# Threshold attention and two feed-forward layers: the first layer's activation as a maximum in its own step, with three h and five y banks, and weight blocks of the second layer decoded one stage later

## The chip, the cores and the metric

The kernel runs on one core of a Trainium2 chip. The metric is device time in microseconds (us) of one execution; lower is better. The kernel before was run three times: 1042.65, 1046.85 and 1047.65 us, so its median is 1046.85 us.

## The reference, cut to what matters

```python
# q, k, v: 4 x 8 heads x 576 x 64; tau = 0.02
scores = scale * q @ k.T
keep   = scores >= max(scores) - tau
x      = softmax(scores where kept) @ v              # 2304 tokens x 512

h = x @ w_in                                          # 512 -> 2048   (first layer)
g = where(h >= 1, h, where(h <= -1, 0, (h + 1)**2 / 4))
x = g @ w_out                                         # 2048 -> 512

h  = x @ w_in2                                        # 512 -> 1024   (second layer)
so = h * softmax(h)
x  = (layernorm(so) * g_ln) @ w_out2                  # 1024 -> 512
```

The four weight matrices arrive as 64-bit floats. The chip's engines work on 32 bits, so every block of 128 x 512 weights is first put together from its two 32-bit words ("decoded"). There are 48 such blocks: 16 of w_in and 16 of w_out of the first layer, 8 of w_in2 and 8 of w_out2.

## The kernel before, in words

Every product is made of two or three matmuls: a tensor is split into a high part (a copy in the matmul's own format) and a low part (the difference). So each activation costs a ScalarE copy for "hi" and a GpSimd subtraction for "lo" before TensorE may use it.

**Attention** (to about 414 us of the profile). The heads are worked in 16 pairs of 9 units each (`attention_unit`, L682); a string in `ORDER` (L68) fixes for each unit what is issued in which order: scores of a later pair ("S", L305) with their row maxima on VectorE (L318), the shifted scores again ("E", L378) with their exponential on ScalarE (L389), the mask on VectorE (L394), the split of the result (L402 ScalarE, L403 GpSimd), the product with v (L426). All loads and copies through DMA go through SyncE's one queue, in program order: `load_kq` (L219 to L229), `stack_k` (L285, L286, L289), `stack_q` (L293), `load_v` (L239, L245), `store_head` (L440, L441), and for batches that are done `load_recip` (L465) into one buffer, which waits for the `normalise` before it (L473). A pair's second head has its `stack_k` DMA in the pair's unit 0, its `stack_q` in unit 2 and its first scores in unit 4.

**Decoding jobs.** The letter "J" in a unit calls `jobs.step`. A job is a generator that does one piece of a block's work per step: load the raw words (L515, 512 KB, SyncE's queue), absolute value (L485, ScalarE), five VectorE instructions (L487, L490, L493, L497, L500), one GpSimd addition (L504). What follows depends on the kind. `to_sbuf` splits the block into hi and lo for TensorE (L531 ScalarE, L533 GpSimd). `to_dram` writes the decoded block to DRAM (L538), from where a later job reads it as plain 32-bit floats (L520, and L529 for w_out2). In the kernel before the attention runs 12 jobs, one begun every 9 units (`JOB_EVERY`) and at most two open at a time: the 8 blocks of the first layer's first quarter, and then rows 0 to 3 of w_out2 through `to_dram`.

**First layer** (about 414 to 832 us). The order is 4 groups of the hidden columns (g), 5 chunks of tokens (c; three of 512, two of 384), 4 steps each (jj): 80 steps n. In step n TensorE does the 12 matmuls of `moe1_in` into one h bank of PSUM, and the 12 of `moe1_out` of two steps before (`LAGO = 2`) into four y banks, one for each 128 output columns. Between them lies `moe1_act`, in two parts:

```python
nc.vector.tensor_scalar(cl, ps, 1.0, -1.0, op0=ALU.min, op1=ALU.max)                                  # L757
nc.scalar.activation(out=ps, in_=ps, func=ACTF.Relu, bias=mone[:, 0:1], scale=1.0)                    # L758
nc.scalar.activation(out=cl, in_=cl, func=ACTF.Square, bias=half[:, 0:1], scale=0.5)                  # L759
yield
nc.vector.tensor_tensor(cl, cl, ps, op=ALU.add)                                                       # L761
nc.scalar.copy(gh, cl)                                                                                # L762
nc.gpsimd.tensor_tensor(gl, cl, f32(gh), op=ALU.subtract)                                             # L763
```

The first part of step n is issued in step n; the second part is issued in step n + 1, behind the first part of that step (L1009). So gh and gl of step n - 2, which `moe1_out` (L779) reads in step n, are made in step n - 1, behind the clamp of step n - 1. In each step `jobs.step` is called up to twice, ahead of the clamp (L1006) and after `moe1_out` and the stores of y (L1028). The jobs of this stage are the next quarter's 8 blocks, then two further `to_dram` blocks (`plan`, L970): 10 in each of the first three groups, at most three open; the last group prepares the second layer's weights. `finish` empties the list at the end of each group.

**Second layer** (about 832 to 1037 us): `moe2_in` (L821) into two h banks, the norm (`moe2_ln`), a transposition through DRAM, and `moe2_out` (L932).

PSUM has eight banks: in the first layer four are a rotating set for h, four are y0 to y3.

Of the kernel before, what the change touches and what calls it, by code (L numbers as in the profile page):

```python
# [9 lines left out]
F32 = mybir.dt.float32  # L10
# [11 lines left out]
def kernel(  # L22
# [39 lines left out]
    T_A, T_B = -16, -10  # L62
    S_UNITS = (-10, -9, -7, -7, -6, -5, -4, -3, -3, -2)
    TURN_AT = 3
    JOB_EVERY = 9


    ORDER = (  # L68
# [51 lines left out]
    one = const.tile([P, 1], F32, name="one")  # L120
    half = const.tile([P, 1], F32, name="half")
    warm = const.tile([P, 1], F32, name="warm")
    mone = const.tile([P, 1], F32, name="mone")
    tau_sb = const.tile([P, 1], F32, name="tau_sb")
    tau_abs = const.tile([P, 1], F32, name="tau_abs")
    ntau = const.tile([P, 1], F32, name="ntau")
# [37 lines left out]

    def setup():
        nc.vector.memset(half, 0.5)
        nc.vector.memset(mone, -1.0)
        make_identity(nc, ident)
        nc.vector.memset(scale2[0:D], 1.0)
        nc.vector.tensor_scalar(  # L170
            scale2[D:P], tau_sb[D:P], 0.0, float(D) ** -0.5, op0=ALU.is_ge, op1=ALU.mult
        )
        nc.vector.tensor_scalar(ntau, tau_sb, -1.0, None, op0=ALU.mult)
        nc.vector.tensor_tensor(tau_abs, tau_sb, ntau, op=ALU.max)
        nc.vector.tensor_tensor(ntau, tau_sb, ntau, op=ALU.min)
# [364 lines left out]
    class Jobs:  # L540
# [2 lines left out]


        def __init__(self, todo, every, depth):
            self.todo, self.depth = [(t, every) for t in todo], depth
            self.live, self.now, self.next, self.begun = [], 0, 0, 0

        def add(self, todo, every):
            self.todo += [(t, every) for t in todo]  # L550

        def step(self, kinds="asb", many=1):
            for job in list(self.live):
                if job[1] > self.now or job[2] and (job[2] not in kinds or job[2] != "a" and many <= 0):
                    continue
                many -= job[2] in ("s", "b")
                n = next(job[0], None)
                if n is None:
                    self.live.remove(job)
                else:  # L560
                    job[1:3] = [self.now + n[0], n[1]]
            if self.todo and self.now >= self.next and len(self.live) < self.depth:
                make, every = self.todo.pop(0)
                g = make()
                n = next(g)
                self.live.append([g, self.now + n[0], n[1], self.begun])
                self.begun += 1
                self.next = self.now + every
            self.now += 1

        def finish(self):
            while self.todo or self.live:
                self.step()

    fine, WAIT, AFTER_ADD = [True], [4], [2]
# [59 lines left out]
    nc.scalar.activation(out=warm, in_=one, func=ACTF.Exp)  # L635
    load_kq(0)
    setup()
    jobs = Jobs(parts(("in1", 0), ("out1", 0)) + ahead_out2(0, 1, 2, 3), JOB_EVERY, 2)
    LAGV = 3
    first_, last_, pe_, act_, late_ = {}, {}, {}, {}, {}  # L640
    by_letter = {"F": first_, "L": last_, "P": pe_, "A": act_, "T": late_}
# [82 lines left out]
    def x_split(c, kk):  # L724
# [4 lines left out]
        nc.scalar.copy(hi, xv)  # L729
        (nc.gpsimd if c else nc.vector).tensor_tensor(lo, xv, f32(hi), op=ALU.subtract)  # L730

    h_ps = {}
    g_t = {}

    def moe1_in(c, j):
        hi, lo = wg_t["in1", j // JG]
        f = slice((j % JG) * P, (j % JG) * P + P)
        ps = ps_h.tile([P, T], F32, tag="h", name="h1")[:, 0 : size(c)]
        xh, xl = x_t[c]
        for kk in range(KD):  # L740
            for n, (a, m) in enumerate(((hi, xh), (lo, xh), (hi, xl))):
                nc.tensor.matmul(  # L742
                    ps,
                    lhsT=a[:, kk, f],
                    rhs=m[:, kk, :],
                    start=(n == 0 and kk == 0),
                    stop=(n == 2 and kk == KD - 1),
                )
        h_ps[c, j] = ps

    def moe1_act(c, j):
        n = size(c)
        ps = h_ps.pop((c, j))
        cl = g_p.tile([P, T], F32, tag="cl", name="cl", bufs=CL)[:, 0:n]
        gh = g_p.tile([P, T], F32R, tag="gh", name="gh", bufs=LAGO + 1)[:, 0:n]
        gl = g_p.tile([P, T], F32R, tag="gl", name="gl", bufs=LAGO + 1)[:, 0:n]
        nc.vector.tensor_scalar(cl, ps, 1.0, -1.0, op0=ALU.min, op1=ALU.max)  # L757
        nc.scalar.activation(out=ps, in_=ps, func=ACTF.Relu, bias=mone[:, 0:1], scale=1.0)  # L758
        nc.scalar.activation(out=cl, in_=cl, func=ACTF.Square, bias=half[:, 0:1], scale=0.5)  # L759
        yield  # L760
        nc.vector.tensor_tensor(cl, cl, ps, op=ALU.add)  # L761
        nc.scalar.copy(gh, cl)  # L762
        nc.gpsimd.tensor_tensor(gl, cl, f32(gh), op=ALU.subtract)  # L763
        g_t[c, j] = (gh, gl)
        yield
# [3 lines left out]
    def moe1_out(c, j):  # L769

        gh, gl = g_t.pop((c, j))
        hi, lo = wg_t["out1", j // JG]
        jj = j % JG
        if jj == 0:
            y_ps[c] = [ps_y.tile([P, T], F32, tag=f"y{d}", name="y1")[:, 0 : size(c)] for d in range(KD)]
        for d in range(KD):
            ds_ = slice(d * P, (d + 1) * P)
            for n, (a, m) in enumerate(((hi, gh), (lo, gh), (hi, gl))):
                nc.tensor.matmul(  # L779
                    y_ps[c][d],  # L780
                    lhsT=a[:, jj, ds_],
                    rhs=m,
                    start=(jj == 0 and n == 0),
                    stop=(jj == JG - 1 and n == 2),
                )
# [27 lines left out]
    def moe2_in(i):  # L813
        r = slice(i % YT * P, i % YT * P + P)
        yh, yl = (t[:, :, r] for t in x_t["y", i // YT])
        ps = [ps_h.tile([P, T], F32, tag="h", name="h") for g in range(2)]
        n = 0
        for kk in range(KD):
            for a, s in ((yh, 0), (yh, 1), (yl, 0)):
                for g in range(2):  # L820
                    nc.tensor.matmul(  # L821
                        ps[g], lhsT=a[:, kk, :], rhs=wg_t["in2", g][s][:, kk, :],
                        start=(n < 2), stop=(n >= 6 * KD - 2),
                    )
                    n += 1
        h2_ps[i] = ps
# [72 lines left out]
    def moe2_tr(i):  # L899
        _, so = ln_t.pop(i)  # L900
        t = wg_pool[1].tile([P, KD, 512], F32R, tag="wg", name="ln").rearrange("p k t -> p (k t)")
        hi, lo = t[:, 0:FF2], t[:, FF2 : 2 * FF2]
        for g in range(2):
            o = slice(T * g, T * g + T)
            ps = ps_y.tile([P, T], F32, tag=f"y{g}", name="lt")
            for f in range(KD):
                r = slice(f * P, f * P + P)
                nc.tensor.transpose(ps[:, r], so[:, T * g + f * P : T * g + f * P + P], ident)
            nc.scalar.copy(hi[:, o], ps)
            nc.vector.tensor_tensor(lo[:, o], ps, f32(hi[:, o]), op=ALU.subtract)  # L910
        lt_t[i] = [v.rearrange("p (f t) -> p f t", t=P) for v in (hi, lo)]
# [14 lines left out]

    def moe2_out(i):
        hi, lo = lt_t.pop(i)
        ps = ps_y.tile([P, DM], F32, tag=f"y{2 + i % 2}", name="o")
        terms = [(hi, f, m) for f in range(KF2) for m in range(2)] + [(lo, f, 0) for f in range(KF2)]  # L930
        for n, (a, f, m) in enumerate(terms):
            nc.tensor.matmul(  # L932
                ps, lhsT=a[:, f, :], rhs=wg_t["out2", f // 4][m][:, f % 4, :], start=(n == 0), stop=(n == len(terms) - 1)
            )
        o = g_p.tile([P, DM], F32, tag="cl", name="o", bufs=CL)
        nc.scalar.copy(o, ps)
        for r, rows in out_rows(i):
            nc.sync.dma_start(rows, o[r, :])
# [12 lines left out]
        if 0 <= u - NU + X_FIRST < KD:  # L951
            x_split(0, u - NU + X_FIRST)
    scores_ps.close()
    ps_h = ctx.enter_context(tc.tile_pool(name="ps_h", bufs=4, space=PSUM))
    for u in range(NU, NU + LAGV + 2):
        attention_unit(u)
        if u - NU in IN_EARLY:
# [6 lines left out]
    if RAW3:  # L964
# [3 lines left out]
    nc.sync.dma_start(g_sb, g_ln.rearrange("(f p) -> p f", p=P))  # L968
    order = [(g, c, jj) for g in range(NG) for c in range(NCH) for jj in range(JG)]
    plan = [  # L970
        parts(("in1", 1), ("out1", 1)) + ahead_out2(4, 5),
        parts(("in1", 2), ("out1", 2)) + ahead_out2(6, 7),
        parts(("in1", 3), ("out1", 3)) + ahead_in2(*IN2_AHEAD),
        parts(("in2", 0), ("in2", 1)),
        parts(("out2", 0)),
        parts(("out2", 1)),
    ]
    begin = {(0, 0, 2): 0, (1, 0, LAGO): 1, (2, 0, LAGO): 2, (3, 0, LAGO): 3, (3, 1, 0): 4, (3, 2, 0): 5}
    jobs = Jobs([], 0, 3)
    fine[0], WAIT[0], AFTER_ADD[0] = False, 2, 1  # L980
# [7 lines left out]
    for n in range(len(order) + LAGO):  # L988
# [3 lines left out]
        if n < len(order):  # L992
            g, c, jj = order[n]
            if order[n] in begin:
                if jj == LAGO:
                    jobs.finish()
                jobs.add(plan[begin[order[n]]], EVERY[begin[order[n]]])
            if (g, c, jj) == (0, 0, 2):
                recips(bl)
            if (g, c) == (0, 1):  # L1000
# [5 lines left out]
                jobs.step(many=9)  # L1006
            act.append(moe1_act(c, j))
            next(act[n])
        if 0 < n <= len(order):  # L1009
            next(act[n - 1])  # L1010
        go, co, jo = order[n - LAGO] if n >= LAGO else (0, 0, 0)
        if n >= LAGO:
            moe1_out(co, JG * go + jo)
# [12 lines left out]
            next(ln[i2])  # L1026
        if n < len(order):
            jobs.step(many=9)  # L1028
            if g == 0 and 4 < n <= 4 + NPAIR:
                normalise(bl, n - 5, nc.vector)  # L1030
            for m in range(x_done(n), x_done(n + 1)):
# [69 lines left out]
```

## Time and profile before

| | us |
|---|---|
| median of 3 runs (lowest, highest) | 1046.85 (1042.65, 1047.65) |
| the profiled execution, its own time | 1043.3 |
| its span, first to last instruction | 1041.5 |
| attention, 28.0 to 414.6: length, TensorE busy | 386.6, 347.84 |
| first layer, 420.2 to 832.0: length, TensorE busy | 411.8, 397.51 |
| second layer, 849.0 to 1037.0: length, TensorE busy | 188.0, 187.98 |

Length minus busy time is time in which TensorE had no matmul under way. In the attention that is 38.8 us, in the first layer 14.3 us, in the second layer 0.0. The profiled execution's own time is 1.8 us more than its span, and 3.55 us less than the median of the three runs.

### The profile page before, as it was taken

The page shows a single profiled execution, that of the slowest core. Times are in us where ns is not written, and L with a number is a line of the kernel's source. Part 1 is how long each engine was busy: PE and PEld are TensorE (multiplying, and loading weights), DVE is VectorE, ACT ScalarE, POOL GpSimd, SP SyncE. Part 2 cuts the span into 40 slices and gives each one's busy share as a digit, 9 for nine tenths or more (in the row PEclk, how much of TensorE's full clock was granted, in tenths as well). Part 3 has the DMA queues.
Part 4 walks back from the last instruction along what each step waited for, and adds up shares of the span by engine and source line. Part 5 has one row for each costly group of instructions (what it writes and reads, how often), then busy time and mean ns, then how long its engine had stood idle before and what let it go on. Part 6 is the DMA issues. An engine that isn't in the chain of part 4 may idle for free.

```text
span 1041.5 us, 15175 instructions
## 1 busy us (share of the span) xinstructions
PE 969.5 (93%) x5232; PEld 841.7 (81%) x5232; DVE 732.1 (70%) x1133; ACT 535.3 (51%) x1006; POOL 598.0 (57%) x569
## 2 busy tenths in 40 slices
PE   4899899889979998999999999999999999999998
PEld 3788888788878897767887888788888988888886
DVE  3788888868877775588747875787567556666662
ACT  2666666756756666645443443444344534344433
POOL 6577778967786776657524552555256823344332
PEclk9999999989999999999999999999999999999999
DMA  6555556555755520321121112111211104444443
GB/s 155 136 136 135 124 136 160 136 122 131 184 145 126 132 70 24 91 84 59 33 71 61 42 41 81 51 51 41 91 41 51 56 7 132 108 121 127 122 131 91
DMA packets 89885, 99.89 MB, mean 96 GB/s; under 512 B 50032, under 2 KB 62640, under 8 KB 89808
## 3 DMA queue, kind: packets, MB, share of 16 engines
q1 hardware_dynamic: 89424, 98.76, 36.5%
q8 instruction: 41, 0.67, 0.3%
q14 instruction: 36, 0.29, 0.1%
q10 hardware_dynamic: 384, 0.16, 0.1%
HBM read 55.13 MB, written 15.88 MB: 68 GB/s over the span
## 4 chain that ended last, share of the span: by engine, by line
PE 54%; issue 13%; DVE 12%; POOL 10%; ACT 6%; DMA 3%; SPq 2%; ACTq 0%; POOLq 0%; DVEq 0%
PE y L779 10%; PE h L742 10%; PE o L932 10%; PE h L821 9%; PE av L426 6%; PE zt L378 5%; PE sc L305 3%; DVE e L394 3%; POOL gl L763 3%; POOL dec_a L504 2%; POOL plo L403 2%; POOL wg L533 2%; ACT e L389 2%; DVE mcol L318 2%; DMA q_st<-lo 1%
## 5 line engine op out<-in xcount | busy, mean ns | idle before, releaser
L403 POOL TENSOR_TENSOR plo<-e,phi 128x576 fp32r<-128x576 f32 x144 | 206.2, 1438 | 80.7 <-ACT phi L402 79.5
L763 POOL TENSOR_TENSOR gl<-cl,gh 128x512 fp32r<-128x512 f32 (+1 forms) x80 | 96.9, 1211 | 189.4 <-ACT gh L762 156.0
L779 PE MATMUL y<-gh,wg 128*128 128x512 f32 (+1 forms) x640 | 187.6, 374 | 4.1 <-ACT gh L762 4.1
L742 PE MATMUL h<-xh,wg 128*128 128x512 f32 (+1 forms) x640 | 185.8, 371 | 2.0 <-DVE e L394 2.0
L394 DVE SCALAR_TENSOR_TENSOR e<-zt,ntau,e 128x576 f32<-128x576 f32 x144 | 116.6, 810 | 64.9 <-ACT e L389 64.7
L758 ACT ACTIVATE h<-h,mone 128x512 f32<-128x512 f32 (+1 forms) x80 | 49.5, 619 | 198.8 <-DVE cl L757 198.6
L389 ACT ACTIVATE e<-zt 128x576 f32<-128x576 f32 x144 | 93.7, 651 | 96.6 <-PE zt L378 81.1
L779 PEld LDWEIGHTS y<-gh,wg 128*128 128x128 f32 x640 | 117.9, 188 | 24.1 <-ACT gh L762 7.8
L742 PEld LDWEIGHTS h<-xh,wg 128*128 128x128 f32 x640 | 119.0, 189 | 19.2 <-DVE e L394 2.3
L779 PE MATMUL y<-gl,wg 128*128 128x512 f32 (+1 forms) x320 | 122.0, 381 | 10.2 <-POOL gl L763 10.2
L318 DVE TENSOR_REDUCE mcol<-sc 128x1 f32<-128x576 f32 x160 | 116.7, 747 | 10.4 <-PE sc L305 10.4
L757 DVE TENSOR_SCALAR cl<-h 128x512 f32<-128x512 f32 (+1 forms) x80 | 50.8, 635 | 102.0 <-PE h L742 69.0
L742 PE MATMUL h<-xl,wg 128*128 128x512 f32 (+1 forms) x320 | 118.8, 371 | 0.0
L932 PE MATMUL o<-wg,ln 128*128 128x512 f32 x432 | 103.2, 395 | 0.0
L821 PE MATMUL h<-wg,y 128*128 128x512 f32 x432 | 101.2, 390 | 0.0
L402 ACT CAST phi<-e 128x576 fp32r<-128x576 f32 x144 | 96.3, 669 | 2.1 <-DVE e L394 1.9
L932 PEld LDWEIGHTS o<-wg,ln 128*128 128x128 f32 x432 | 81.0, 188 | 19.2
L821 PEld LDWEIGHTS h<-wg,y 128*128 128x128 f32 x432 | 81.0, 188 | 17.0
L896 POOL TENSOR_TENSOR ln<-land,ln 128x1024 fp32r<-128x1024 f32 x16 | 38.5, 2408 | 92.2 <-ACT ln L895 86.4
L378 PE MATMUL zt<-q_st,k_both 128*128 128x288 f32 x320 | 76.9, 322 | 10.4 <-ACT mt L345 5.2
L305 PE MATMUL sc<-k_both,q_st 128*128 128x288 f32 x320 | 73.4, 312 | 13.1 <-DMA q_st<-lo 8.7
L779 PEld LDWEIGHTS y<-gl,wg 128*128 128x128 f32 x320 | 60.1, 188 | 27.3 <-POOL gl L763 19.1
(109 smaller groups left out, 1940.4 us busy)
## 6 DMA issues: line engine op xcount, KB each, us to landing
raw<-in_moe_w_in_dram SPq DMA_DIRECT2D x24, 512.0 KB
raw<-in_moe_w_out_dram SPq DMA_DIRECT2D x24, 512.0 KB
k_both<-q_st SPq DMA_DIRECT2D x30, 288.0 KB
sq<-so SPq DMA_DIRECT2D x64, 128.0 KB
land<-sq SPq DMA_DIRECT2D x16, 512.0 KB
k_both<-lo SPq DMA_DIRECT2D x32, 144.0 KB
q_st<-lo SPq DMA_DIRECT2D x32, 144.0 KB
x<-xs SPq DMA_DIRECT2D x32, 144.0 KB
```

Source lines behind the costliest of these rows:

```text
L305: nc.tensor.matmul(ps[:, c, 0:HS], lhsT=st[j][i][r, n * P : n * P + P], rhs=kk[j][i][r, o + c * HS : o + (c + 1) * HS], start=(st is q_st) ...
L318: nc.vector.tensor_reduce(mc[:, n : n + 1], sc_ps.pop((h, n))[:, :, 0:HS], axis=AXES.XY, op=ALU.max, negate=True)
L378: nc.tensor.matmul(ps[:, c, 0:HS], lhsT=st, rhs=mv[:, c * HS : (c + 1) * HS], start=(m == 0), stop=(m == len(todo) - 1),)
L389: nc.scalar.activation(out=e, in_=st_ps[u][:, :, 0:HS], func=ACTF.Exp)
L394: nc.vector.scalar_tensor_tensor(out=e, in0=st_ps.pop(u)[:, :, 0:HS], scalar=ntau[:, 0:1], in1=e, op0=ALU.is_ge, op1=ALU.mult)
L402: nc.scalar.copy(hi, e)
L403: (nc.vector if u - NU in LO_DVE or u < NU - UNITS and u % UNITS in LO_UNITS else nc.gpsimd).tensor_tensor(lo, e, f32(hi), op=ALU.subtract)
L742: nc.tensor.matmul(ps, lhsT=a[:, kk, f], rhs=m[:, kk, :], start=(n == 0 and kk == 0), stop=(n == 2 and kk == KD - 1),)
L763: nc.gpsimd.tensor_tensor(gl, cl, f32(gh), op=ALU.subtract)
L779: nc.tensor.matmul(y_ps[c][d], lhsT=a[:, jj, ds_], rhs=m, start=(jj == 0 and n == 0), stop=(jj == JG - 1 and n == 2),)
L821: nc.tensor.matmul(ps[g], lhsT=a[:, kk, :], rhs=wg_t["in2", g][s][:, kk, :], start=(n < 2), stop=(n >= 6 * KD - 2),)
L932: nc.tensor.matmul(ps, lhsT=a[:, f, :], rhs=wg_t["out2", f // 4][m][:, f % 4, :], start=(n == 0), stop=(n == len(terms) - 1))
```

## The change

In the first layer's activation the Relu and the addition become one maximum. The second part of the activation is issued at the end of its own step. The PSUM banks are split into three for h and five for y, and the y banks rotate: a chunk's four take the bank that was left free first. In the second layer an even tile takes one h and one y bank. The attention keeps only the 8 blocks of the first layer's first quarter, one begun every 14 units. The w_out2 blocks 0 to 3 are decoded in the first layer instead: its groups 0, 1 and 2 get lists of 3, 3 and 4 spare `to_dram` jobs behind the 8 that must be done, and `finish` no longer waits for spare jobs that are still open.

```diff
-    JOB_EVERY = 9
+    JOB_EVERY = 14
...
-            self.todo, self.depth = [(t, every) for t in todo], depth
+            self.todo, self.depth = [(t, every, True) for t in todo], depth
...
         def finish(self):
-            while self.todo or self.live:
+            while any(t[2] for t in self.todo) or any(job[3] for job in self.live):
                 self.step()
...
-    jobs = Jobs(parts(("in1", 0), ("out1", 0)) + ahead_out2(0, 1, 2, 3), JOB_EVERY, 2)
+    jobs = Jobs(parts(("in1", 0), ("out1", 0)), JOB_EVERY, 2)
...
+    NHB, NYB = 3, KD + 1
+    turns = [0, 0]
+
+    def bank(what, n, nm):
+        return (ps_h if what == "h" else ps_y).tile([P, T], F32, tag=f"{what}{n}", name=nm)
+
+    def y_bank(n, nm):
+        return bank("y", (turns[1] + n) % NYB, nm)
...
-        ps = ps_h.tile([P, T], F32, tag="h", name="h1")[:, 0 : size(c)]
+        ps = bank("h", turns[0] % NHB, "h1")[:, 0 : size(c)]
+        turns[0] += 1
...
         nc.vector.tensor_scalar(cl, ps, 1.0, -1.0, op0=ALU.min, op1=ALU.max)
-        nc.scalar.activation(out=ps, in_=ps, func=ACTF.Relu, bias=mone[:, 0:1], scale=1.0)
         nc.scalar.activation(out=cl, in_=cl, func=ACTF.Square, bias=half[:, 0:1], scale=0.5)
         yield
-        nc.vector.tensor_tensor(cl, cl, ps, op=ALU.add)
+        nc.vector.tensor_tensor(cl, cl, ps, op=ALU.max)
...
-            y_ps[c] = [ps_y.tile([P, T], F32, tag=f"y{d}", name="y1")[:, 0 : size(c)] for d in range(KD)]
+            y_ps[c] = [y_bank(d, "y1")[:, 0 : size(c)] for d in range(KD)]
+            turns[1] += KD
...
-        ps = [ps_h.tile([P, T], F32, tag="h", name="h") for g in range(2)]
+        ps = [bank("h", (turns[0] + n) % NHB, "h") for n in ((1, 2) if i % 2 else (0,))]
+        if i % 2 == 0:
+            ps.append(y_bank(0, "h"))
...
-        parts(("in1", 1), ("out1", 1)) + ahead_out2(4, 5),
-        parts(("in1", 2), ("out1", 2)) + ahead_out2(6, 7),
-        parts(("in1", 3), ("out1", 3)) + ahead_in2(*IN2_AHEAD),
+        parts(("in1", 1), ("out1", 1)),
+        parts(("in1", 2), ("out1", 2)),
+        parts(("in1", 3), ("out1", 3)),
...
+    spare = [ahead_out2(0, 1, 2), ahead_out2(3, 4, 5), ahead_in2(*IN2_AHEAD) + ahead_out2(6, 7), [], [], []]
...
+                jobs.add(spare[at_], EVERY[at_], False)
...
             act.append(moe1_act(c, j))
             next(act[n])
-        if 0 < n <= len(order):
-            next(act[n - 1])
...
         if n < len(order):
             jobs.step(many=9)
+            next(act[n])
```

## Rows read from the trace of the kernel before

**Rows 1.** The page: busy time, share of the span and instructions of each engine.

```profile
PE 969.5 (93%) x5232; PEld 841.7 (81%) x5232; DVE 732.1 (70%) x1133; ACT 535.3 (51%) x1006; POOL 598.0 (57%) x569
```

**Rows 2.** Windows: length, busy PE, PEld, DVE, ACT, POOL, granted clock, DMA share, GB/s.

```profile
28.00:414.60 386.60, 347.84 (x2383) 320.54 (x2384) 306.23 (x398) 253.13 (x480) 289.19 (x280) 0.98 0.53 127
420.20:832.00 411.80, 397.51 (x1861) 337.42 (x1861) 290.91 (x414) 185.55 (x338) 218.53 (x172) 1.00 0.19 59
849.00:1037.00 188.00, 187.98 (x826) 153.25 (x824) 113.82 (x276) 76.36 (x151) 63.84 (x49) 1.00 0.43 114
```

**Rows 3.** Waits of PE between 414 and 850 us: us, times, longest.

```profile
PE y L779 <- POOL gl L763: 10.2, 21, 0.9
PE y L779 <- ACT gh L762: 4.1, 9, 0.8
```

**Rows 4.** Timeline of one such wait: start, us, engine, line, [idle before].

```profile
498.39 0.55 DVE L487 TENSOR_SCALAR dec_a<-dec_a 128x512 f32<-128x512 f32 x1
...
503.27 0.69 DVE L500 SCALAR_TENSOR_TENSOR raw<-raw 128x512 f32<-128x512 uint32 x1
503.88 0.55 DVE L757 TENSOR_SCALAR cl<-h 128x384 f32<-128x384 f32 x1
...
504.47 0.56 ACT L758 ACTIVATE h<-h,mone 128x384 f32<-128x384 f32 x1 [3.71 <-DVE cl L757]
504.95 0.60 ACT L759 ACTIVATE cl<-cl,half 128x384 f32<-128x384 f32 x1
505.45 0.50 ACT L762 CAST gh<-cl 128x384 fp32r<-128x384 f32 x1
506.01 0.62 PE L779 MATMUL y<-gh,wg 128*128 128x384 f32 x2 [0.24 <-ACT gh L762]
...
507.09 0.44 PE L779 MATMUL y<-gl,wg 128*128 128x384 f32 x1 [0.47 <-POOL gl L763]
507.37 0.52 PE L779 MATMUL y<-gh,wg 128*128 128x384 f32 x2
507.72 0.34 PE L779 MATMUL y<-gl,wg 128*128 128x384 f32 x1
```

**Rows 5.** Windows of attention pairs, columns as in rows 2.

```profile
71.02:95.10 24.08, 21.89 (x154) 20.08 (x153) 20.86 (x27) 16.29 (x32) 18.59 (x18) 1.00 0.57 133
...
344.74:366.34 21.60, 20.37 (x149) 19.20 (x148) 15.78 (x22) 14.66 (x29) 15.22 (x16) 1.00 0.49 114
366.34:388.34 22.00, 20.67 (x149) 19.47 (x149) 16.72 (x23) 14.47 (x29) 15.76 (x16) 1.00 0.30 76
...
192.20:221.80 29.60, 24.37 (x155) 22.40 (x154) 19.18 (x28) 16.52 (x31) 21.40 (x22) 0.88 0.62 148
...
293.45:321.83 28.38, 23.28 (x155) 21.56 (x154) 19.23 (x27) 16.00 (x30) 20.17 (x21) 0.94 0.71 174
```

**Rows 6.** SyncE's queue, issues in order of time: start, us, line, transfer.

```profile
191.11 1.68 SPq L465 DMA_DIRECT2D rb<-rec  x2
...
199.21 0.53 SPq L515 DMA_DIRECT2D raw<-in_moe_w_out_dram  x1
199.83 0.65 SPq L285 DMA_DIRECT2D k_both<-q_st  x1
...
204.57 0.48 SPq L441 DMA_DIRECT2D x<-xs  x1
205.97 0.48 SPq L293 DMA_DIRECT2D q_st<-lo  x1
```

**Rows 7.** Windows at the two long waits and behind them, columns as in rows 2.

```profile
205.74:209.87 4.13, 0.00 (x2) 0.03 (x1) 1.41 (x2) 2.24 (x5) 3.46 (x3) 0.81 0.75 180
209.87:215.10 5.23, 5.23 (x22) 5.16 (x23) 1.51 (x2) 1.44 (x3) 1.38 (x5) 0.50 0.74 161
306.62:310.63 4.01, 0.00 (x0) 0.03 (x1) 1.60 (x2) 2.24 (x5) 3.38 (x4) 1.00 0.82 193
310.63:314.10 3.47, 3.47 (x15) 3.44 (x16) 0.76 (x1) 0.00 (x0) 1.62 (x4) 0.51 0.80 175
```

More of the change, by code (lines that the diff above doesn't have):

```diff
@@ L122 @@
     warm = const.tile([P, 1], F32, name="warm")
-    mone = const.tile([P, 1], F32, name="mone")
     tau_sb = const.tile([P, 1], F32, name="tau_sb")
@@ L166, in setup @@
         nc.vector.memset(half, 0.5)
-        nc.vector.memset(mone, -1.0)
         make_identity(nc, ident)
@@ L545, in __init__, with add @@
         def __init__(self, todo, every, depth):
-            self.todo, self.depth = [(t, every) for t in todo], depth
-            self.live, self.now, self.next, self.begun = [], 0, 0, 0
-        def add(self, todo, every):
-            self.todo += [(t, every) for t in todo]
+            self.todo, self.depth = [(t, every, True) for t in todo], depth
+            self.live, self.now, self.next = [], 0, 0
+        def add(self, todo, every, must=True):
+            self.todo += [(t, every, must) for t in todo]
         def step(self, kinds="asb", many=1):
@@ L562, in step @@
             if self.todo and self.now >= self.next and len(self.live) < self.depth:
-                make, every = self.todo.pop(0)
+                make, every, must = self.todo.pop(0)
                 g = make()
                 n = next(g)
-                self.live.append([g, self.now + n[0], n[1], self.begun])
-                self.begun += 1
+                self.live.append([g, self.now + n[0], n[1], must])
                 self.next = self.now + every
@@ L904, in moe2_tr @@
             o = slice(T * g, T * g + T)
-            ps = ps_y.tile([P, T], F32, tag=f"y{g}", name="lt")
+            ps = y_bank(1 + g, "lt")
             for f in range(KD):
@@ L928, in moe2_out @@
         hi, lo = lt_t.pop(i)
-        ps = ps_y.tile([P, DM], F32, tag=f"y{2 + i % 2}", name="o")
+        ps = y_bank(3 + i % 2, "o")
         terms = [(hi, f, m) for f in range(KF2) for m in range(2)] + [(lo, f, 0) for f in range(KF2)]
@@ L953 @@
     scores_ps.close()
-    ps_h = ctx.enter_context(tc.tile_pool(name="ps_h", bufs=4, space=PSUM))
+    ps_h = ctx.enter_context(tc.tile_pool(name="ps_h", bufs=1, space=PSUM))
     for u in range(NU, NU + LAGV + 2):
@@ L996 @@
                     jobs.finish()
-                jobs.add(plan[begin[order[n]]], EVERY[begin[order[n]]])
+                at_ = begin[order[n]]
+                jobs.add(plan[at_], EVERY[at_])
+                jobs.add(spare[at_], EVERY[at_], False)
             if (g, c, jj) == (0, 0, 2):
```

## The prediction

> **What bounds the kernel now.** I read the page first. TensorE (PE) is busy 93% of the span [rows 1], so the kernel can lose time only where PE waits, and the windows show where that is [rows 2]. The second layer has no gap: 187.98 us busy in 188.0. The change touches the order of its banks and nothing that PE waits for there, so I give it no part of the sum. The first layer has 411.80 - 397.51 = 14.3 us without a matmul, the attention 386.60 - 347.84 = 38.8 us.
>
> The waits say what ends the gaps of the first layer [rows 3]: 21 waits for gl (10.2 us) and 9 for gh (4.1 us), 14.3 us together, the whole gap. One of them in order of time shows why [rows 4]. Five VectorE (DVE) instructions of a decoded block run from 498.39 to 503.96. The clamp of step n stands behind them and starts at 503.88. The addition for step n - 1 stands behind that clamp, Relu and Square of step n stand ahead of the copy to gh on ScalarE (ACT), and so gh of step n - 1 comes at 505.45, when PE is done with all that it had. The value PE lacks is one whose inputs have been ready for a step; it waits in the queues behind work of the next step.
>
> For the attention I compared pairs of units [rows 5]. A pair with one block in decoding takes 24.08 us with DVE busy 20.86. The pairs at 344.74 and 366.34, after the last block, take 21.60 and 22.00 us with DVE busy 15.78 and 16.72. Two pairs are far longer, 29.60 and 28.38 us. In each of them PE stands still for about 4 us and then runs at a granted clock of 0.50 and 0.51 (1.2 GHz of 2.4) for 5.23 and 3.47 us [rows 7]. What comes late there is a stack DMA: SyncE's queue issues one DMA after the other from 191.11, when it came free of its wait for the normalised batch; a raw load (199.21) stands directly ahead of the stack of k (199.83), and the stack of q, which overwrites what that reads, goes out 6.14 us later at 205.97 [rows 6].
>
> **The change, part by part.**
>
> *Second part at the end of its own step, maximum, no Relu.* Issued in step n instead of n + 1, gh and gl have some 1.5 steps of PE's time until they are read, where they had one. In a chunk of 384 a step is about 4.2 us (24 matmuls, two of them in the 0.35 us between the starts of 507.37 and 507.72), so gh gains over 4 us against a lateness of 0.24 and 0.47 us in rows 4; the longest wait of the stage is 0.9 us [rows 3]. Relu (0.56 us in rows 4) leaves ACT's part of this chain; the maximum stands where the addition stood, and no row has one, so I bound it by the addition's cost (0 more) and one Relu (0.56 us more); either is inside the 4 us, and I take 0. The waits are 14.3 us. After each, the first matmuls are longer: 0.62 against 0.52 and 0.44 against 0.34 [rows 4], so 0.1 us for each of 30 waits, 3 us more. Upper bound 17.3 us. Lower bound 0, if DVE itself is what is late. I take three quarters, **-13 us**: the margin is several times the lateness, but DVE now holds a maximum that waits for Square, with the next step's decoding and clamp queued behind it, and PE waits for that clamp's result two steps on.
>
> *Banks.* The h bank of step n - 3 must be free in step n; its reader is now issued at the end of step n - 3, two steps ahead. The y banks' release appears in no wait of PE [rows 3], so the fifth brings 0. What hides a late release is the 2.1 us of `moe1_in` in front; if that cover goes, a store of y of about one Relu's length would be seen at 19 chunk changes, some 10 us, which the slower rival takes in.
>
> *Four blocks out of the attention.* For each: five instructions on DVE, one on ACT, one on GpSimd (POOL), a load and a store on SyncE's queue. Pairs with and without a block differ by 24.08 - 21.60 = 2.48 or 24.08 - 22.00 = 2.08 us [rows 5]. The later pairs also lack most of the loads of q and k, so 2.48 is the upper bound; the lower is 0, if those loads make all of it. DVE's difference of 4.1 to 5.1 us a pair speaks for decoding, so I take 1.9 a block: **-7.6 us** (0 to -9.9). The other 8 blocks stay, one every 14 units; I price them unchanged.
>
> *The two long pairs.* They exceed 24.08 by 5.5 and 4.3 us, 9.8 in all [rows 5], the bound. The jobs' new spacing puts loads at units 54 and 68 and none between, so the raw load of row 199.21 is gone, and in the second long pair, where a load begins in unit 96, the store of a decoded block and the load of unit 97 are gone. SyncE's queue is then about 0.6 us earlier in both, and 512 KB no longer stand ahead of the stack of k. I estimate the stack of q some 1.5 us earlier in each: its next limit is its place behind the rows of a finished head, which go out from 204.57 to 205.05 now [rows 6]. That is -3.1 us. The slow clock costs half of 5.23 and of 3.47 us, 4.3 in all [rows 7]. PE had stood still 2.5 us already when it fell in the first case (by its 0.81 in the window of the wait) and 4.0 in the second, so waits of 2.5 us lie between; I take a fifth, -0.9. Together **-4 us** (0 to -9.8).
>
> The Trainium skill says of this gate (TensorE: Matmul & The Clock Gate, What's actually happening) that "the default state is throttled, and activity releases the throttle", in words: the clock follows how busy PE has just been. By that a shorter wait could keep the full clock altogether, and the sum would be 3.4 us lower; no row here has a wait of that length.
>
> *Four blocks into the first layer.* DVE there is busy 290.91 of 411.80 us [rows 2]; by the pairs a block is at most 5.1 us, so 20 us more on 121 idle. What hides it is the new slack in the chain. They come behind each group's 8 needed blocks, and the needed ones begin when they began. 0 in the sum; up to +20 if the cover is gone.
>
> **The sum** is -13 - 7.6 - 4 = -24.6 us. The profiled execution took 1043.3, which gives 1018.7; it stands 3.55 below the median of 1046.85, from which the same gain gives 1022.2. I say 1020.
>
> **Rivals.**
>
> *One stage only.* The pairs' difference is the missing loads, or PE's earlier arrival turns into longer waits for the same DMAs: SyncE's chain from 191.11 hangs on POOL, not on PE [rows 6]. Then the attention gives about nothing and the first layer 13, or the other way round 11.6: about 1031. For it: two things changed between the pairs compared. Against it: DVE was fuller by just the block's work.
>
> *All of it.* -17.3 - 9.9 - 9.8 = -37: 1006. It needs both long waits short enough that the clock stays at 2.4 GHz. For it: PE never fell below it in the first layer, whose waits are at most 0.9 us. Against it: the queue's 5 us of lateness from 191.11 is not touched.
>
> *DVE becomes the bound of the first layer: slower.* Each of 80 steps now has one place where DVE stands still until Square is done, 0.60 us and two handings-over, say 0.8 us (an estimate from rows 4: 503.88 plus 0.55 to 504.47 and on): 64 us. With 20 us of decoding, 290.91 + 64 + 20 = 375 of the 397.5 us in which PE must work. It decides where decoding is dense enough for DVE to need more than PE in a stretch of several steps. If then the 20 us of the blocks come onto the path on top of the present waits, and the attention gives nothing, it is 1043 + 20 = 1063. Against it: most such halts are filled by the decoding issued between clamp and maximum.
>
> *Nothing gained.* The waits stay, with the maximum late in place of the addition, and the long pairs take what the four blocks leave: about 1043.
>
> **How the numbers follow.** Forecast 0.56, one stage only 0.22, all of it 0.12, nothing 0.06, slower 0.04. The range 1007 to 1035 takes in the forecast, one stage only, and part of the third. Half a per cent, about 5 us, is what a measurement of this kernel can tell from no change: faster by more 0.90, within it 0.06, slower 0.04.
>
> **What would show it.** Right: in the first layer the waits of PE for gh and gl under 5 us, and the stage from the first `moe1_out` to the second layer under 400 us; attention pairs of 22 to 23.5 us where none is long; the two waits near 2.5 us. Wrong: a wait of PE for gl that remains with DVE full, the pairs still 24 us, or the long waits unchanged with the slow clock behind them. The second layer should stay at 188 us.

## The result, and the profile after

The changed kernel takes 1006.96 us, median of four executions (1004.87 to 1010.71), against 1046.98 us for the kernel before in the same comparison: a ratio of 0.963 (95% interval 0.9588 to 0.9673), faster by 40 us. The forecast was 1020 with a range of 1007 to 1035, so the time lies at the low end of the range, 0.04 us outside it. The direction was right, and the size was 40 us where 24.6 were summed.

The page's line of busy time, after:

```profile
PE 962.0 (95%) x5232; PEld 850.7 (84%) x5232; DVE 711.2 (70%) x1132; ACT 499.3 (49%) x926; POOL 598.1 (59%) x569
```

PE's busy time fell by 7.5 us from [rows 1] for the same 5232 matmuls, the span by 32.6. Windows of the three stages after, columns as in rows 2:

```profile
28.00:405.30 377.30, 349.94 (x2392) 326.43 (x2393) 279.62 (x379) 250.14 (x476) 280.05 (x276) 0.99 0.53 122
410.90:800.50 389.60, 389.11 (x1862) 340.31 (x1861) 296.05 (x434) 154.02 (x264) 227.38 (x177) 1.00 0.23 70
817.50:1004.00 186.50, 186.50 (x825) 153.14 (x823) 113.58 (x276) 76.32 (x151) 63.79 (x49) 1.00 0.42 115
```

The first layer has 0.5 us left without a matmul; in [rows 2] it had 14.3. The wait of PE that is left and, below the dots, the wait of DVE that the change adds, between 410 and 800 us, after: us, times, longest:

```profile
PE y L788 <- POOL gl L771: 0.4, 1, 0.4
...
DVE cl L769 <- ACT cl L767: 23.4, 28, 1.2
```

Thirty waits have become one. The change also takes a wait of DVE away, one that the prediction did not count. There are two `cl` buffers, and with the second part issued a step late the clamp had to wait for the gl of an earlier step to be done with its buffer. DVE in the first layer before (420 to 832 us):

```profile
DVE cl L757 <- POOL gl L763: 24.2, 17, 2.2
```

After, there is no such wait in the stage: DVE stands still for Square 23.4 us, and no longer 24.2 us for gl. The timeline after shows a step in a chunk of 384 with a block in decoding, as in [rows 4] (start, us, engine, line, [idle before]):

```profile
480.16 0.54 DVE L766 TENSOR_SCALAR cl<-h 128x384 f32<-128x384 f32 x1
480.63 1.05 DVE L495 TENSOR_SCALAR raw<-dec_a 128x512 uint32<-128x512 uint32 x1
480.80 0.62 ACT L767 ACTIVATE cl<-cl,half 128x384 f32<-128x384 f32 x1 [2.77 <-DVE cl L766]
481.71 0.69 DVE L498 SCALAR_TENSOR_TENSOR raw<-raw 128x512 f32<-128x512 uint32 x1
482.32 0.55 DVE L769 TENSOR_TENSOR cl<-cl,h 128x384 f32<-128x384 f32 x1
482.96 0.52 ACT L770 CAST gh<-cl 128x384 fp32r<-128x384 f32 x1 [1.54 <-DVE cl L769]
483.55 1.02 POOL L771 TENSOR_TENSOR gl<-cl,gh 128x384 fp32r<-128x384 f32 x1 [2.16 <-ACT gh L770]
...
484.29 0.52 PE L788 MATMUL y<-gh,wg 128*128 128x384 f32 x2
...
484.64 0.43 PE L788 MATMUL y<-gl,wg 128*128 128x384 f32 x1
```

gl is complete at 484.57, and the first matmul that reads it begins at 484.64, 0.07 us later. In this step the margin of 4 us that the prediction counted on is used up: three instructions of the decoding had put the clamp off. Steps like this are few. When each of the 80 ends of gl is set against the first matmul that reads it, the median margin is 3.51 us, where it was 1.12 before; it is under 0.3 us in 3 steps (0.05, 0.06 and 0.07, all in the first group), where it was in 27. DVE does two instructions of the decoding between clamp and maximum, while Square runs, so here the maximum waits for nothing.

For the stages I set the first start of `moe1_out` and of `moe2_in` as borders. "After, again" is the same changed kernel in a later comparison (experiment 5). The profile of "after" is that of the slowest of its four executions (1010.71 us), the one of "after, again" that of the fastest of its four (1001.86).

| us | before | after | after, again | said |
|---|---|---|---|---|
| start to first `moe1_out` | 420.2 | 410.9 | 402.1 | -11.6 |
| to first `moe2_in` | 412.0 | 389.6 | 389.6 | -13 |
| to the end | 209.3 | 208.4 | 208.5 | 0 |
| span | 1041.5 | 1008.9 | 1000.1 | -24.6 |

The two profiles of the changed kernel differ in the attention alone, largely at its start: PE goes at about half its pace there in the one and not in the other (last section). Against the profile with a start like that of before, the stages gave -18.1, -22.4 and -0.9, together 41.4 us (the medians differ by 39 to 40).

The pairs of the attention, columns as in rows 5: an ordinary one and the two long ones, after:

```profile
80.43:102.91 22.48, 21.27 (x154) 20.01 (x153) 17.51 (x25) 15.19 (x29) 16.41 (x18) 1.00 0.60 140
...
171.25:197.86 26.61, 23.14 (x154) 21.52 (x153) 18.03 (x26) 16.34 (x31) 20.13 (x20) 0.94 0.60 136
...
288.22:314.48 26.26, 23.11 (x153) 21.44 (x152) 18.39 (x25) 16.39 (x31) 20.99 (x21) 0.94 0.61 143
```

Ordinary pairs went from about 24.08 [rows 5] to about 22.5 us. The long ones are shorter but there, and the first has come a pair earlier (it began at 192.20, now at 171.25). What holds it is again the stack of q, after, SyncE's queue in order of time:

```profile
175.38 1.10 SPq L463 DMA_DIRECT2D rb<-rec  x2
176.54 0.58 SPq L513 DMA_DIRECT2D raw<-in_moe_w_out_dram  x1
177.21 0.25 SPq L438 DMA_DIRECT2D sums<-xs  x1
177.50 0.48 SPq L439 DMA_DIRECT2D x<-xs  x1
178.03 0.59 SPq L291 DMA_DIRECT2D q_st<-lo  x1
```

and the windows of the two waits and of what follows each, after, columns as in rows 7:

```profile
181.13:183.50 2.37, 0.00 (x1) 0.03 (x1) 1.60 (x3) 2.24 (x5) 1.74 (x3) 1.00 1.11 218
184.60:188.02 3.42, 3.42 (x17) 3.39 (x16) 1.28 (x2) 1.62 (x3) 2.54 (x6) 0.50 0.46 110
298.01:300.08 2.07, 0.01 (x2) 0.04 (x1) 0.82 (x1) 1.94 (x4) 2.07 (x3) 1.00 0.83 227
300.65:304.06 3.41, 3.41 (x17) 3.36 (x15) 0.76 (x1) 0.66 (x2) 2.38 (x5) 0.50 0.82 181
```

The waits are 2.37 and 2.07 us long (4.13 and 4.01 in [rows 7]), and a stretch at 0.50 of the clock still follows each.

### The profile page after: what moved, and what is told of

It reads as the page before. It is cut to its first block, busy times and chain, and to the rows that moved or that the text cites. A ratio compares the mean times of both kernels' runs of the same rounds, so it can differ in the third digit from the quotient of the medians.

```text
span 1008.9 us, 15104 instructions
## 1 busy us (share of the span) xinstructions
PE 962.0 (95%) x5232; PEld 850.7 (84%) x5232; DVE 711.2 (70%) x1132; ACT 499.3 (49%) x926; POOL 598.1 (59%) x569
## 4 chain that ended last, share of the span: by engine, by line
PE 81%; ACT 5%; DVE 4%; issue 3%; POOL 3%; SPq 2%; DMA 1%; ACTq 1%; POOLq 0%; DVEq 0%
PE y L788 19%; PE h L750 19%; PE o L943 10%; PE h L832 10%; PE av L424 8%; PE zt L376 7%; PE sc L303 5%; DVE e L392 3%; ACT e L387 2%; PE tr L260 2%; POOL plo L401 1%; ACT phi L400 1%; ACTq L344 1%; DMA q_st<-lo 1%; ACT mt L343 1%
## 5 line engine op out<-in xcount | busy, mean ns | idle before, releaser
L771 POOL TENSOR_TENSOR gl<-cl,gh 128x512 fp32r<-128x512 f32 (+1 forms) x80 | 100.1, 1251 | 168.8 <-ACT gh L770 89.8
L767 ACT ACTIVATE cl<-cl,half 128x512 f32<-128x512 f32 (+1 forms) x80 | 54.4, 680 | 98.0 <-DVE cl L766 97.6
L770 ACT CAST gh<-cl 128x512 fp32r<-128x512 f32 (+1 forms) x80 | 46.3, 579 | 112.4 <-DVE cl L769 102.0
```

## The experiments

Runs 1 to 4 share one series of the kernel before (median 1044.64), 5 to 8 another (1044.96), 9 and 10 a third (1045.0), 11 and 12 a fourth (1045.45). Ratios are to these.

**1. The order alone**, in the kernel before.

```diff
-        if 0 < n <= len(order):
-            next(act[n - 1])
...
             jobs.step(many=9)
+            next(act[n])
```

> The kernel before with one edit: the second part of the activation is issued at the end of its own step (Relu and addition stay, banks and jobs stay). Theory: the place of issue alone takes TensorE's waits for gh and gl away: under 2 us of them left, 17 to 22 us less than the kernel before, all in the first layer. Rival (the Relu on ScalarE is the late link): waits stay above 8 us, at most 7 us less. Rival (banks): nothing gained, within 3 us of before.

Measured: 1025.3 us, 0.9817 (0.9792 to 0.9842). The first layer takes 392.4 us, 19.6 less. PE's waits there:

```profile
PE y L779 <- ACT x L794: 2.3, 2, 1.4
PE y L779 <- POOL gl L763: 0.3, 1, 0.3
```

The waits for gh and gl are gone but for 0.3 us. What is left hangs on ScalarE, which still does the Relu: it is late with the copy that empties a y bank.

**2. The maximum alone**, still one step late, in the kernel before.

```diff
-        nc.scalar.activation(out=ps, in_=ps, func=ACTF.Relu, bias=mone[:, 0:1], scale=1.0)
...
-        nc.vector.tensor_tensor(cl, cl, ps, op=ALU.add)
+        nc.vector.tensor_tensor(cl, cl, ps, op=ALU.max)
```

> The kernel before with one edit: no Relu, a maximum in place of the addition, still issued one step later. Theory (place of issue): gh still waits behind the next step's clamp and Square but comes some 0.6 us earlier, and most waits are 0.2 to 0.9 us, so a part goes: waits of 14.3 us fall to 4 to 9 us, 6 to 13 us less. Rival (Relu is the late link): all waits go, 17 to 22 us less. Rival (maximum slower than the addition): within 3 us of before or slower.

Measured: 1033.36 us, 0.9891 (0.9865 to 0.9917). The first layer takes 400.2 us, 11.8 less, with these waits:

```profile
PE y L778 <- POOL gl L762: 5.7, 14, 0.8
PE y L778 <- ACT gh L761: 0.2, 1, 0.2
```

Each edit alone takes over half the gain, and the two overlap: 19.6 + 11.8 = 31.4 against 22.4 in the whole change (which has new banks and four more blocks in this stage besides).

**3. The jobs alone**: blocks moved and spaced as in the change, with the old activation and banks.

```diff
-    JOB_EVERY = 9
+    JOB_EVERY = 14
...
-    jobs = Jobs(parts(("in1", 0), ("out1", 0)) + ahead_out2(0, 1, 2, 3), JOB_EVERY, 2)
+    jobs = Jobs(parts(("in1", 0), ("out1", 0)), JOB_EVERY, 2)
...
+    spare = [ahead_out2(0, 1, 2), ahead_out2(3, 4, 5), ahead_in2(*IN2_AHEAD) + ahead_out2(6, 7), [], [], []]
```

> The kernel before with the jobs of the change alone: 8 blocks in the attention, one every 14 units, the other four as spare jobs in the first layer; activation and banks as before. Theory: attention pairs 22.5 us instead of 24.1, the two long pairs some 3 us shorter each, 10 to 15 us less in the attention; the first layer's chain has no slack there, so its waits grow by 1 to 4 us with four more blocks; 8 to 13 us less in all. Rival (the pairs differ by the missing loads of q and k, not by decoding): pairs stay near 24, at most 4 us less.

Measured: 1038.12 us, 0.9942 (0.9917 to 0.9967), 6.5 us less. The first layer takes 421.5 us, 9.5 more than before. The waits there, and then a window with one of the longer ones (1.64 us for gh, ending at 817.17) and what follows it:

```profile
PE y L778 <- POOL gl L762: 12.6, 26, 0.9
PE y L778 <- ACT gh L761: 6.8, 12, 1.6
```

```profile
815.00:822.00 7.00, 4.89 (x20) 4.25 (x19) 4.01 (x9) 4.31 (x9) 3.58 (x4) 0.76 0.15 37
```

Four blocks in the first layer cost 9.5 us under the old order, in longer waits and one stretch below full clock. This misses the expectation, and it is the price of the cover that the prediction named.

**4. The whole change without the new banks** (four h banks, y0 to y3 fixed).

```diff
-        ps = bank("h", turns[0] % NHB, "h1")[:, 0 : size(c)]
+        ps = ps_h.tile([P, T], F32, tag="h", name="h1")[:, 0 : size(c)]
...
-            y_ps[c] = [y_bank(d, "y1")[:, 0 : size(c)] for d in range(KD)]
+            y_ps[c] = [ps_y.tile([P, T], F32, tag=f"y{d}", name="y1")[:, 0 : size(c)] for d in range(KD)]
```

> The whole change but for the banks: four h banks that rotate and y0 to y3, as before. Theory: banks give nothing, so 37 to 41 us less than the kernel before, as the changed kernel. Rival (rotating y banks free TensorE at chunk changes): 3 us or more short of the changed kernel, with waits of TensorE for the stores of y.

Measured: 1009.52 us, 0.9679 (0.9646 to 0.9711), 35 us less than before, a little short of what was expected. The first layer takes 390.1 us, 0.5 more than with the banks, and the second 209.3. Here too PE has one wait for gl, 0.4 us, in the first layer.

**5 to 8.** The changed kernel again, as the base of the next three (its diff is empty); a block every 9 units; the loads of the reciprocals later; two more blocks in the first layer.

> The changed kernel itself, on the chip of the three runs beside it, as their measure: 36 to 41 us less than the kernel before.

Measured: 1005.76 us, 0.9621 (0.9585 to 0.9656). Its first long wait is of interest: 2.10 us for the same stack of q, but the clock stayed full. The second is 2.11 us long and the clock fell. Windows of this run, the first wait with what follows, then the second, columns as in rows 7:

```profile
175.20:177.30 2.10, 0.01 (x1) 0.03 (x1) 1.61 (x3) 1.96 (x5) 1.47 (x2) 1.00 1.11 220
177.30:185.00 7.70, 7.20 (x51) 6.79 (x52) 4.38 (x6) 3.70 (x8) 7.55 (x9) 1.00 0.32 72
290.92:293.03 2.11, 0.00 (x0) 0.03 (x1) 0.82 (x1) 1.98 (x5) 2.11 (x3) 0.94 0.83 210
293.03:296.45 3.42, 3.42 (x15) 3.39 (x16) 0.76 (x1) 0.26 (x1) 2.89 (x5) 0.54 0.83 181
```

**6. A block every 9 units** in the changed kernel: eight blocks, as dense as before.

```diff
-    JOB_EVERY = 14
+    JOB_EVERY = 9
```

> The changed kernel with one block begun every 9 units again in the attention (8 blocks, so the last load is in unit 61 and not 96). Theory as predicted (every block costs its pair about 1.9 us, whatever the spacing): the pairs with a block go back to 24.1, those behind them to 22, the sum stays: within 3 us of the changed kernel. Rival (a pair has slack, and at one block in 14 units decoding fits into it, at one in 9 it does not): 7 pairs at 24.1 against 22.5, the rest 22.4 at the best: 7 to 12 us more than the changed kernel.

Measured: 1015.57 us, 0.9713 (0.9683 to 0.9742), 9.8 more than the change. Windows of a pair with a block, and of one behind the last block that still has its loads of q and k:

```profile
78.81:102.89 24.08, 21.91 (x153) 20.09 (x153) 20.86 (x27) 16.29 (x31) 18.58 (x19) 1.00 0.56 134
...
274.77:297.16 22.39, 21.17 (x154) 19.99 (x153) 15.55 (x22) 15.20 (x29) 18.06 (x18) 1.00 0.53 127
```

The pair is back at 24.08 us. Without decoding and with the loads it is 22.39: a block at that density costs 1.7 us, and the rest of the 2.48 and 2.08 us in the prediction was the loads missing from the two later pairs of [rows 5]. An ordinary pair of the changed kernel takes 22.48, 0.1 more. A few take longer (23.6 at the most), so the price is better taken from the sum: from the third pair to the fourteenth, without the two long ones, run 5 has 4.2 us more than 22.39 a pair, some 0.5 for each of the eight blocks if they make all of it.

**7. The loads of the reciprocals later**, so that SyncE's queue does not wait for them ahead of the next heads' stacks.

```diff
-    NORM = (13, 5)
+    NORM = ((15, 9), (15, 9), (16, 5))
...
-            o = (b + 1) * NPAIR * UNITS + NORM[0] + NORM[1] * p
+            o = (b + 1) * NPAIR * UNITS + NORM[b][0] + NORM[b][1] * p
...
-            at(late_, o + NORM[1], normalise, b, p, nc.vector if b == 2 else nc.gpsimd)
+            at(late_, o + NORM[b][1], normalise, b, p, nc.vector if b == 2 else nc.gpsimd)
```

> The changed kernel with the loads of the reciprocal sums moved: for the first two batches one every 9 units, in the unit of the load of q and k and behind it in SyncE's queue, for the third one every 5 units from 3 units later. Theory (the long pairs come from SyncE's queue standing at the reciprocal load ahead of the loads of q, k and the stacks): both long pairs fall from 26.5 to about 22.8 us, the waits for q_st and the half clock behind them go, 6 to 9 us less than the changed kernel. Rival (bandwidth of the DMAs, or GpSimd's normalising, is what is late): the long pairs only move or stay, within 2 us of the changed kernel.

Measured: 995.56 us, 0.953 (0.95 to 0.9559), 10.2 less than the change in the same comparison; the profiled executions differ by 6.2. It is the fastest version of this study. SyncE's queue and the window of the pair in which the first long wait was:

```profile
160.51 1.24 SPq L463 DMA_DIRECT2D rb<-rec  x2
...
164.29 0.64 SPq L283 DMA_DIRECT2D k_both<-q_st  x1
...
167.17 0.58 SPq L513 DMA_DIRECT2D raw<-in_moe_w_out_dram  x1
...
171.19 0.54 SPq L291 DMA_DIRECT2D q_st<-lo  x1
```

```profile
161.90:184.40 22.50, 21.23 (x153) 19.84 (x152) 17.86 (x24) 15.97 (x31) 17.70 (x18) 1.00 0.64 157
```

What SyncE's queue waited for at the load of the reciprocals, between 28 and 405 us, in the changed kernel and, in a second fence, in this run:

```profile
SPq L463 <- POOL x L471: 13.9, 5, 4.7
```

```profile
SPq L463 <- POOL x L471: 3.3, 3, 1.8
```

No pair is long any more. The raw load is still there, 4 us ahead of the stack of q, and every block's load with it; what this run changes is the hold of the queue at the reciprocals, which falls from 13.9 to 3.3 us on GpSimd, and that is the cause. The edit does two things at once, though: the loads stand elsewhere in the queue, and the normalising that they wait for comes every 9 units and not every 5 (for the first two batches). Which of the two shortens the hold was not tried apart, and neither was what a raw load close ahead of the stack of q adds to it.

**8. Two more blocks in the first layer** (rows 0 and 3 of w_out2 are decoded twice).

```diff
-    spare = [ahead_out2(0, 1, 2), ahead_out2(3, 4, 5), ahead_in2(*IN2_AHEAD) + ahead_out2(6, 7), [], [], []]
+    spare = [ahead_out2(0, 1, 2, 0), ahead_out2(3, 4, 5, 3), ahead_in2(*IN2_AHEAD) + ahead_out2(6, 7), [], [], []]
```

> The changed kernel with two blocks more in the first layer: rows 0 and 3 of w_out2 are decoded and stored twice, as spare jobs of the first two groups. Theory (the new slack hides decoding there): TensorE's waits in the stage stay under 1 us, at most 2 us more than the changed kernel. Rival (a block costs the first layer what it cost with the old order, 9.7 us for four when the jobs alone were moved): 4 to 6 us more.

Measured: 1009.65 us, 0.9668 (0.9636 to 0.97), 3.9 more than the change, with intervals that overlap; the profiled executions differ by 2.3. The first layer is the same to 0.1 us, 389.6. The extra of the profile is where nobody expected it, in the second layer, 211.0 us, with this wait of PE from 791 us on, where the profile of the changed kernel shows none:

```profile
PE o L943 <- ACT ln L906: 2.0, 2, 1.1
```

Run 7, without the extra blocks, has a wait of the same kind, from 784 us on, and a second layer of 210.0 us:

```profile
PE o L943 <- ACT ln L906: 1.0, 2, 0.7
```

So the six blocks cost the first layer nothing that its length shows, and the late norm need not be theirs. What makes it late is open.

**9. A block every 10 units** (`JOB_EVERY = 10` in the changed kernel).

> The changed kernel with one block begun every 10 units: nearly the density of 9, but the blocks fall on changing units of a pair, as at 14. Theory (density: VectorE's slack in a pair holds some decoding and no more): pairs with decoding 23.4 to 24 us, 5 to 9 us more than the changed kernel. Rival (position: at 9 every block falls on the same, bad units of its pair): pairs stay at 22.5 to 22.9, within 3 us of the changed kernel.

Measured: 1011.85 us, 0.9672 (0.9632 to 0.9711). The pairs lie between 22.75 and 24.08 us, such as this one:

```profile
78.60:102.30 23.70, 21.87 (x155) 20.17 (x155) 18.93 (x26) 16.27 (x32) 18.44 (x19) 1.00 0.58 135
```

So 10 lies between 9 and 14. Whether it is the density of the blocks or the units on which their instructions fall isn't settled by this.

**10. Relu and addition back** in the changed kernel, for the maximum.

```diff
+        nc.scalar.activation(out=ps, in_=ps, func=ACTF.Relu, bias=mone[:, 0:1], scale=1.0)
...
-        nc.vector.tensor_tensor(cl, cl, ps, op=ALU.max)
+        nc.vector.tensor_tensor(cl, cl, ps, op=ALU.add)
```

> The changed kernel with Relu and addition in place of the maximum (place of issue, banks and jobs as changed). Theory (the place of issue gives the slack, the maximum is then inside it): TensorE's waits in the first layer stay under 1.5 us, the stage at 390 to 392 us, at most 3 us more than the changed kernel. Rival (both are needed): the stage above 395 us.

Measured: 1016.23 us, 0.973 (0.9706 to 0.9754), 9 to 10.5 us more than the changed kernel's two medians, where less was expected. The rows give the edit only 2.9 us in the first layer (392.5) and 0.9 in the second (209.4). The rest stands in the attention, which the edit doesn't touch: against run 5's profile the first exponential is 1.0 us later, the first pair 3.8 us longer (25.78 and 22.03; the slow start of the last section) and the first long pair 2.5 us longer (27.33 and 24.80).

**11. The same edit in the kernel of run 7**, to settle that.

> The kernel with the reciprocal loads moved, with Relu and addition back in place of the maximum. With the long pairs gone the attention should vary less. Theory (Relu back costs the first layer 2.9 us and the second 0.9, as the profile of the changed kernel with Relu showed, and the rest of its 10 us was the attention's own variation): ratio to the kernel before 0.955 to 0.958, that is 2 to 5 us more than with the maximum (0.953). Rival (the Relu costs 10 us in some way that the stages don't show): 0.962 or more.

Measured: 1000.89 us, 0.9573 (0.9549 to 0.9598), inside the narrow expectation. The first layer is again 392.5. The ratio is 0.0043 above that of run 7, or 4.5 us, with intervals that just overlap, so the maximum is worth some 3 to 5 us once the order is right, and most of run 10's excess was not the edit's.

**12. The kernel of run 7 without the new banks.**

> The kernel with the reciprocal loads moved, with four h banks and y0 to y3 as before. Theory (banks give 0.6 us in the first layer and 0.9 in the second, as the stages of the run without banks showed): ratio 0.953 to 0.956, at most 3 us more. Rival (banks are worth 3 us or more): 0.957 or more.

Measured: 999.84 us, 0.9557 (0.9539 to 0.9574), inside the expectation. The first layer takes 390.1 us as in run 4, 0.5 more. The ratio is 0.0027 above that of run 7, 2.8 us, with overlapping intervals. What the banks give beyond the 0.5 us can't be told: the second layer takes 208.5 to 210.0 us with them (runs 5 and 7) and 209.3 or 209.4 without.

## Why the prediction was right, and where it was not

**First layer: right mechanism, mis-sized.** Said -13 with a bound of 17.3; measured -22.4. Run 1 shows that the order does it. The bound failed, not only the three quarters. It was the 14.3 us of listed waits plus 0.1 us for each first matmul, and the waits fell by 13.8 (14.3 to 0.5 in the windows), but PE's busy time in the stage fell by a further 397.51 - 389.11 = 8.4 us for the same number of matmuls. The groups of its lines over all 1920 matmuls give 3.2 of these (614.2 to 611.0 us in sum), which is the 0.1 us each that I had added. The other 5 us I read as overlap, which no run isolated: a busy time counts the stretches that two matmuls share once, and after a wait there is nothing to share with. The size fits. In [rows 4] two matmuls start within 0.35 us and one lasts 0.34, so each shares about 0.165 us with the next, and 30 times that is 5.0 us (an estimate). I priced how much longer the matmul behind a wait is, and not that it starts alone. In effect a wait cost 22.2 / 30 = 0.74 us where 0.48 is listed. The margin that takes the waits away was smaller than "over 4 us": 3.51 in the median against 1.12 before, and nothing in three steps of the first group, where decoding holds the clamp up. (Of [rows 4], 505.45 is where the copy to gh starts; it ends at 505.95, just before the matmul at 506.01.)

**Banks: right** within 0.5 us in the first layer.

**Four blocks out of the attention: too low, by a wrong assumption.** Said -7.6. With the long pairs apart, the pairs gave 12.4 us (before against run 5: 16.2 in the sum of all pairs, 3.8 of it in the two long ones). The price of 1.9 a block was near the 1.7 of run 6. What failed is "The other 8 blocks stay, one every 14 units; I price them unchanged": spaced at 14 they cost 0.1 in an ordinary pair, and some 0.5 each over the pairs that are not long. So the pairs gained 12.4 / 1.7, some seven blocks' worth, with four blocks gone.

**The two long pairs: right size, by another way.** Said -4; their excess over an ordinary pair went from 9.9 to 6.1 us in run 5, so -3.8. But I had the queue 0.6 us earlier in the same two pairs. The first moved to the pair before, where another raw load (176.54) goes out behind the held loads and 1.5 us ahead of the stack of q (178.03), with only a finished head's rows between. I had seen that the load of row 199.21 goes and not asked what the new spacing puts behind the next wait for the reciprocals. In the second no raw load stands there any more. Run 7 removes the cause that both share. (The 1.5 us that I gave each make 3.0, not 3.1.) The fifth for the clock (-0.9) is neither right nor wrong: it stayed full once and fell three times in four waits of 2.07 to 2.37 us. The Trainium skill has the clock follow how busy PE has been recently (TensorE: Matmul & The Clock Gate, What's actually happening). That agrees with run 7, where the waits are gone and the pair of the first has 1.00, and it leaves room for run 5's first wait (1.00); for the other three, about as short, it gives no reason why the clock fell.

**Four blocks into the first layer: right, and the condition too.** They cost 0 under the new order: run 10, with Relu and addition, the new order and the four blocks, takes the 392.5 us that run 1 takes without them (392.4; the banks differ too), and run 8 with two more takes the 389.6 of the change. Under the old order they cost 9.5 (run 3), within the 20 that I had set for a lost cover.

**The rivals.** "All of it" named 1006, which is the time measured, but not for its reasons: it wanted the long pairs gone, and they were not. The first layer went past its bound instead. "One stage only" fell, since both stages gave more than their terms. "DVE becomes the bound" fell too: the maximum waited for Square 28 times in 80 steps, 23.4 us in all, where I had estimated 64; PE's waits for gh and gl came to 0.4 us, and against the 23.4 stand the 24.2 us of the clamp's own wait for gl, which had gone uncounted and went. "Nothing gained" fell with the waits.

## What to carry to other kernels

When an engine waits for a value whose inputs were ready long ago, look at what was issued ahead of it on its queue; issuing the value's last steps in its own step, ahead of the next step's work, was worth 19.6 us here, and four to six more blocks in that stage then showed no cost. Price a short wait of TensorE above its listed time (0.74 us for 0.48 here), since the matmul behind it is longer and, by the estimate above, the overlap of the matmuls around it goes too. Don't price background work by the block when its spacing changes: one every 9 units cost 1.7 us, one every 14 some 0.1 to 0.5. Look for a margin where the background work is densest, not in the mean: here the median was 3.51 us and the least 0.05. When a load is moved in an in-order DMA queue, look for the place where that queue is held and ask what will now stand behind it; moving the loads at which the queue was held, and the work that they wait for, gave 10 us beyond the whole change.

## What the hardware showed that I had not expected

**A slow start.** In most of the profiled executions, of several kernels, PE goes at about half its pace up to some 45 us. The windows from 33 to 45 us of the kernel before and, in a second fence, of the one after:

```profile
33.00:45.00 12.00, 10.82 (x78) 10.00 (x77) 8.82 (x13) 8.27 (x15) 8.41 (x9) 1.00 0.62 143
```

```profile
33.00:45.00 12.00, 11.74 (x49) 10.50 (x48) 6.75 (x9) 5.34 (x10) 4.25 (x3) 1.00 0.57 130
```

49 matmuls in the time of 78, with PE busy throughout. By the end of the first pair this costs 5.9 us (first exponential at 32.57 and not 29.63, first pair 25.03 and not 22.07 us). After's row says 1.00; the row of run 10 shows the clock with as few matmuls (x52): 0.57. Of the fourteen profiles nine have 49 to 59 matmuls in these 12 us, one has 69 (run 1), and four have 76 to 78 (before and runs 5, 7 and 8). The changed kernel has had both starts (run 5 has 76), so it belongs to the execution and not to the change. What decides it is open, and it is why a stage was compared with the same stage above, and not one profile's span with another's.

**Equal waits, unequal clocks.** In one profile (run 5) a wait of 2.10 us left the clock at 1.00 and one of 2.11 us was followed by 3.42 us at 0.54. In run 3 the clock fell behind a wait of 1.64 us, shorter than the one that left it at 1.00 (its window has 0.76). The length of the wait alone does not decide.
